# Full attention's value products in two row halves with two banks of sums, and row maxima of two heads at once in the score slots

## The chip, the cores and the metric

The kernel runs on one core of one Trainium2 chip. The metric is the device time of one execution in microseconds, lower is better. Five engines work side by side, each through its own instructions in order: TensorE (PE, matmuls into PSUM), VectorE (DVE), ScalarE (ACT), GpSimd (POOL) and SyncE (SP, which issues most transfers).

## The reference, cut to what matters

Four layers follow each other on x, a 2048 x 512 matrix; each adds its result to x.

```python
x = x + _A_ref(_layernorm(x, axis=-1), A_wq, A_wk, A_wv, A_wo)
x = x + _B_ref(_layernorm(x, axis=-1), B_wq, B_wk, B_wv, B_wo, B_beta)
x = x + _A_ref(...)    # the same two layers once more
x = x + _B_ref(...)
```

Layer A is full attention of 32 heads of 16 channels over all 2048 keys, with one key head and one value head for all of them. Layer B cuts the 2048 positions into four segments of 512; within a segment it does causal attention of 32 heads (p = softmax(logits + mask), a_dot = p @ v), and mixes that with a read from a memory matrix that the earlier segments filled.

## The kernel before, in words

**Layer A.** A unit is four heads (two pairs) of one block of 512 queries, against the 16 tiles of 128 keys; there are 8 units a block, 4 blocks, 2 layers. For each key tile, `a_units` computes the scores of one head pair at a time with `by_pairs` (8 matmuls, 49 rows by 32 columns, heads in the lower and the upper half of the array's rows, each half into a bank of its own), ScalarE takes the exponential of the 128 x 1024 result (L743) into a buffer `pa`, and one key tile later `a_pv` multiplies with the values: four f32 matmuls of 128 rows by 17 columns, one for each head, in four strips of columns, which sum over the key tiles in the one bank `pva`. After a unit's last key tile VectorE transposes `pva` (L772), divides and stores.

**Layer B.** For each segment (a block) and each of 8 units of four heads: `b_inputs` projects queries and keys, `b_rowmax` finds for every query row the maximum of its masked scores (a set: 4 heads by 4 query tiles, of 128 to 512 columns), with VectorE reading the scores from PSUM (L968); `guard_rows` transposes the maxima (L674), scales them and sends them into the query tile, so that they are subtracted in the scores proper. `b_attend` then computes the scores, exponentials (L1007, into `pb`) and value products `b_pv` (sums in the bank `pvb`). The last block of the second layer B uses `b_rowmax_masked`.

**PSUM** has eight banks. `layout` names, for each stage, what is shared out of them: `sc`, pairs of banks for scores ("score slots"), `m`, single banks for row maxima, `r`, single banks for projections and transposes. Each is a `Ring`: jobs take its slots in turn, and a job waits until its slot has been read. While both layers run (stage "ab") there are two score slots, one `m` bank and one `r` bank; `pva` is bank 6 and `pvb` bank 7.

**The order.** All work is written as generators that yield when they next can go on. `weave` runs layer A's units of one block (`a_units`) beside the other layer's work on the block before (`side`), and `par` runs parts of `side` beside each other. They choose by estimated times (`pe`, `on`), with an estimated 130 ns (`DRAIN`) for a change between matmuls of different shapes on the array ("full", "cols", "rows"). A scheduler that keeps close to this order then lays out each engine's instructions. So a change of a cost, of a bank or of a shape's name moves instructions through the whole program.

Of the kernel before, what the change touches and what calls it, by code (L numbers as in the profile page):

```python
# [29 lines left out]
F32 = mybir.dt.float32  # L30
F32R = mybir.dt.float32r
BF16 = mybir.dt.bfloat16
# [3 lines left out]
ALU = mybir.AluOpType  # L36
AX = mybir.AxisListType

P = 128
# [50 lines left out]
def net_kernel(ctx, tc, x_in, a_wq, a_wk, a_wv, a_wo, b_wq, b_wk, b_wv, b_wo, b_beta, cst, out):  # L90
    nc = tc.nc
    V, A, G = nc.vector, nc.scalar, nc.gpsimd
# [3 lines left out]
    def together(first, *a, **k):  # L96

        if first:
            nc.tensor.matmul(*a, **k)  # L99
        else:  # L100
            with tc.high_priority(offset=400):
                tc.keep_in_program_order(nc.tensor.matmul(*a, **k))  # L102
# [52 lines left out]
    def tmp(n, shape, dt, tag):  # L155
        return pools[n].tile(shape, dt, tag=tag, name=nm(tag))
# [93 lines left out]
    xh = st([P, 4, 512], F32R, "xh")  # L250
    xl = st([P, 4, 512], F32R, "xl")
    bank = ps_1.tile([P, 8, 512], F32, tag="bank", name="bank")
    pva, pvb = bank[:, 6, :], bank[:, 7, :]
    V.memset(bank[:, 6:8, :], 0.0)


    srcs = {"Aq": (a_wq, 1), "Ao": (a_wo, 0), "Bq": (b_wq, 1), "Bk": (b_wk, 1), "Bv": (b_wv, 0), "Bo": (b_wo, 0)}
# [446 lines left out]
    def a_units(units):  # L704

        def gate(f, n, k1):
            return 0.0 if f <= phase[0] or (f == phase[0] + 1 and (n == 0 or k1 < 16)) else 1e18

        def load(ui):
            L, _, b, n, _, _ = units[ui]
            return a_load(L, b, n) if L["qr"][b][n // 2] < 1e17 else None

        pend = None
        nxt = load(0)
        for ui, (L, f, b, n, k0, k1) in enumerate(units):
# [12 lines left out]
            for kt in range(k0, k1):  # L730
                pe_, te = [], []
                for u in range(2):
                    yield Need(lambda: max(need, rings["sc"].ready(), L["kr"][kt // 4], gate(f, n, k1)), form)
                    ring = rings["sc"]
                    k, sc = ring.take()
                    ks = L["kst"][:, kt * P:(kt + 1) * P]
                    if L["exact"]:
                        for i in range(2):
                            by_columns(i == 0, sc[:, i, :], ks[0:98], q[0:98, 2 * u + i, :], start=True, stop=True)
                    else:  # L740
                        by_pairs(sc, ks.bitcast(F16), q[:, u, :])
                    x = tmp(4, [P, 2, 512], F32, "pa")
                    A.activation(x, sc, AF.Exp, scale=scale)  # L743
                    ring.free[k] = on("act", pe(432 if L["exact"] else 216, form), 946)
                    pe_.append(x)
                    te.append(ring.free[k] + HOP)
                if kt == k0 + 1 or (kt == k0 and k1 - k0 == 1):
                    nxt = load(ui + 1) if ui + 1 < len(units) else None
                if kt == max(k0, k1 - 3) and (b, n) in L["part"]:
                    L["old"] = tmp(2, [P, 16, 32], F32, "xn")  # L750
                    nc.sync.dma_start(L["old"], L["part"].pop((b, n)))
                if pend is not None:
                    yield Need(lambda: max(pend[-1], pva_free[0] if pend[1] else 0.0), "cols")
                    a_pv(*pend)
                pend = (L, kt == k0, kt, pe_, (f, b, n, k0, k1), kt == k1 - 1, max(te))
        yield Need(lambda: max(pend[-1], pva_free[0] if pend[1] else 0.0), "cols")
        a_pv(*pend)

    a_ob = {}
# [1 line left out]
    def a_pv(L, first, kt, x, unit, last, _):  # L761
        f_, b, n, k0, k1 = unit
        gone[f_] = gone.get(f_, 0) + 1
        t, p = divmod(n, 2)
        for j in (2, 3, 0, 1):
            together(j == 2, pva[32 * j:32 * j + 17, :], lhsT=L["va"][:, kt, 0:17], rhs=x[j // 2][:, j % 2, :],
                     start=first, stop=last)
        e = pe(848, "cols")
        if not last:
            return  # L770
        t1 = tmp(2, [P, 16, 32], F32, "t1")
        V.transpose(t1.rearrange("p a b -> p (a b)"), pva)  # L772
# [171 lines left out]
    def b_rowmax(n, need, exact=False):  # L944

        q, k = (qx, kx) if exact else (qb[n % 3], kb[n % 3])
        m = tmp(2, [P, 4, 4], F32, "m")
        jobs = [[(3, j)] for j in range(4)] + [[(2, j), (0, j)] for j in range(4)] + [[(1, 0), (1, 2)], [(1, 1), (1, 3)]]
        for job in jobs:
            yield Need(lambda: max(need, rings["m"].ready()), "cols" if exact else "rows")  # L950
            ring = rings["m"]
            s, ps = ring.take()
            o_ = 0
            for qt, j in job:
                nk = (qt + 1) * P
                if exact:
                    by_columns(o_ == 0, ps[:, o_:o_ + nk], q[0:96, j, qt * P:(qt + 1) * P], k[0:96, j, 0:nk],
                               start=True, stop=True)
                else:
                    u, i = divmod(j, 2)  # L960
                    by_pairs(ps[:, o_:o_ + nk], q[:, u, qt * P:(qt + 1) * P], k[:, u, 0:nk], 48, (i,))
                o_ += nk
                e = pe(cols(nk), "cols" if exact else "rows")
            o_ = 0
            for qt, j in job:
                nk = (qt + 1) * P
                mo = tmp(1, [P, 512], BF16, "mo")
                V.tensor_tensor_reduce(out=mo[:, 0:nk], in0=ps[:, o_:o_ + nk], in1=maskq[:, 512 - nk:512],  # L968
                                       op0=ALU.add, op1=ALU.max, scale=1.0, scalar=-3.0e38,
                                       accum_out=m[:, j, qt:qt + 1])  # L970
                o_ += nk
                e = on("dve", e, 65 + 1.05 * nk)
            ring.free[s] = e
        yield rings["m"].ready
        gr[n] = guard_rows(m, q, rings["m"], exact)

    b_ob = {}
    pvb_free = [0.0]
# [280 lines left out]
```

## Time and profile before

| | |
|---|---|
| times of three runs | 3223.19, 3226.74 and 3234.41 us; median 3226.74 |
| span of the profiled execution | 3225.5 us (the only time that is known of this execution; it lies among the three) |
| TensorE busy | 2971.5 us, 92% |
| ScalarE busy | 2351.4 us, 73% |
| VectorE busy | 1548.4 us, 48% |
| GpSimd busy | 401.0 us, 12% |
| mean granted TensorE clock | 0.982 |

Busy time counts the time in which at least one instruction of an engine ran. Matmuls overlap, and their ends are modelled, so that the distance from start to start says more of TensorE than its busy time. In the rows of groups, the number behind the bar is the busy time in us, then the mean ns of one instruction, then the idle time of the engine ahead of them and who ended it. In the timeline a row begins with its start and its length in us. In the windows a row has the stretch, its length, then busy time (and count) of PE, PEld, DVE, ACT and POOL, the granted clock, and the DMA's share and rate.

### The profile page before, as it was taken

What the parts mean: (1) busy time and instruction counts of PE and PEld (TensorE: products, weight loads), DVE (VectorE), ACT (ScalarE), POOL (GpSimd) and SP (SyncE); (2) the same over time, 40 slices, a digit from 0 to 9 for tenths busy, and PEclk for the clock granted to TensorE, in tenths of its full rate; (3) what the DMA queues carried; (4) which work ended last, traced back from release to release, by engine and by line L of the source; (5) the groups of instructions that cost most, each with busy time, mean ns of one, the idle gap of its engine ahead of it and who ended that gap; (6) DMA issues with size and microseconds to landing.
All of it is one profiled execution on the core that took longest, in us unless ns stands there. A gap on an engine that the chain in (4) does not pass through costs nothing.

```text
span 3225.5 us, 99506 instructions
## 1 busy us (share of the span) xinstructions
PE 2971.5 (92%) x43522; PEld 1097.9 (34%) x43522; DVE 1548.4 (48%) x4423; ACT 2351.4 (73%) x2583; POOL 401.0 (12%) x569
## 2 busy tenths in 40 slices
PE   6988999999999999999999999899999999999997
PEld 3411333334332343333323323333323233332543
DVE  6601345444554446544455534564446433554365
ACT  3599787866888668876788787777587876888322
POOL 2200111021100220002200011110211012100111
PEclk9999999999999999999999999999999999999968
DMA  4300121022110221102311222221211024210511
GB/s 119 115 25 22 52 60 44 18 73 71 49 41 13 75 86 41 38 22 76 92 41 45 70 80 73 72 55 31 87 48 56 16 78 137 63 42 17 168 51 30
DMA packets 138493, 193.04 MB, mean 60 GB/s; under 512 B 29664, under 2 KB 97088, under 8 KB 138048
## 3 DMA queue, kind: packets, MB, share of 16 engines
q1 hardware_dynamic: 118912, 121.56, 12.8%
q0 software_dynamic: 19136, 65.02, 7.0%
q8 instruction: 343, 5.62, 0.7%
q14 instruction: 102, 0.84, 0.1%
HBM read 126.46 MB, written 60.03 MB: 58 GB/s over the span
## 4 chain that ended last, share of the span: by engine, by line
PE 55%; ACT 25%; issue 7%; DVE 6%; DMA 3%; POOL 2%; SPq 0%; ACTq 0%; POOLq 0%; DVEq 0%
PE bank L99 34%; ACT pa L743 22%; PE bank L441 15%; PE bank L102 5%; ACT pb L1007 3%; POOL w L183 1%; DVE mo L968 1%; PE bank L501 1%; DMA wst<-in_B_wk_dram 1%; DMA wst<-in_B_wv_dram 1%; DVE m L939 0%; DVE w L285 0%; POOL parts L537 0%; DVE qf L519 0%; DVE t L1018 0%
## 5 line engine op out<-in xcount | busy, mean ns | idle before, releaser
L743 ACT ACTIVATE pa<-bank 128x1024 f32<-128x1024 f32 x2048 | 1967.6, 1035 | 476.3 <-PE bank L102 462.3
L99 PE MATMUL bank<-pa,va 128*17 128x512 f32 x2048 | 1063.3, 601 | 46.7 <-ACT pa L743 28.8
L102 PE MATMUL bank<-pa,va 128*17 128x512 f32 x6144 | 1077.1, 601 | 0.0
L99 PE MATMUL bank<-qa,kst 49*32 49x512 f16 x2048 | 713.0, 382 | 89.7 <-ACT pa L743 55.3
L102 PE MATMUL bank<-qa,kst 49*32 49x512 f16 x14336 | 785.1, 386 | 0.7 <-DVE xt L815 0.7
L968 DVE CUSTOM_DVE_ANT_0 mo<-bank,maskq 128x256 bf16<-128x256 f32 (+3 forms) x896 | 436.8, 488 | 454.8 <-PE bank L102 444.3
L1007 ACT ACTIVATE pb<-bank 128x1024 f32<-128x1024 f32 (+2 forms) x384 | 329.0, 882 | 160.3 <-PE bank L102 158.9
L99 PE MATMUL bank<-qkb 48*32 48x128 f16 (+7 forms) x1536 | 374.7, 305 | 56.6 <-DVE m L968 20.5
L102 PE MATMUL bank<-qkb 48*32 48x512 f16 (+7 forms) x6656 | 396.0, 308 | 0.0
L99 PEld LDWEIGHTS <-kst 49*32 49x32 f16 x2048 | 144.8, 89 | 669.2 <-issue 658.7
L441 PE MATMUL bank<-xh,w 128*128 128x512 f32 x832 | 298.0, 419 | 10.3 <-DVE w L315 4.7
L102 PEld LDWEIGHTS <-kst 49*32 49x32 f16 x14336 | 208.9, 89 | 213.8 <-issue 206.7
L183 POOL TENSOR_SCALAR w<-wst 128x512 fp32r<-128x512 f32 x160 | 112.0, 700 | 1200.6 <-PE bank L441 1051.0
L441 PE MATMUL bank<-w,xh 128*128 128x512 f32 x752 | 251.3, 414 | 8.4 <-DVE xl L509 7.4
L99 PEld LDWEIGHTS bank<-pa,va 128*17 128x17 f32 x2048 | 116.9, 95 | 363.0 <-issue 224.4
L99 PEld LDWEIGHTS <-qkb 48*32 48x32 f16 (+1 forms) x1536 | 128.4, 92 | 328.0 <-issue 289.7
L772 DVE STREAM_TRANSPOSE t<-bank 128x512 f32<-128x512 f32 x88 | 62.9, 715 | 338.4 <-PE bank L102 338.1
L441 PEld LDWEIGHTS bank<-xh,w 128*128 128x128 f32 x832 | 161.6, 195 | 80.1 <-issue 35.1
L99 PE MATMUL bank<-pb,vb 128*17 128x512 f32 (+3 forms) x512 | 183.1, 447 | 4.3 <-ACT pb L1007 4.1
L102 PE MATMUL bank<-pb,vb 128*17 128x512 f32 (+3 forms) x1536 | 186.1, 447 | 0.0
L102 PEld LDWEIGHTS <-qkb 50*32 50x32 f16 (+1 forms) x6656 | 144.6, 92 | 103.2 <-issue 100.4
L441 PE MATMUL bank<-xl,w 128*128 128x512 f32 x416 | 169.7, 408 | 0.0
(162 smaller groups left out, 2835.0 us busy)
## 6 DMA issues: line engine op xcount, KB each, us to landing
sb<-parts SPq DMA_DIRECT2D x128, 128.0 KB
qkb<-sb SPq DMA_DIRECT2D x256, 64.0 KB
x<-xt SPq DMA_DIRECT2D x48, 256.0 KB
xt<-x SPq DMA_DIRECT2D x48, 256.0 KB
qa<-sd SPq DMA_DIRECT2D x176, 66.0 KB
wd<-w POOLq DMA_DIRECT2D x20, 512.0 KB, 3.8
w<-wd POOLq DMA_DIRECT2D x18, 512.0 KB, 5.2
xt<-in_A_x_dram SPq DMA_DIRECT2D x32, 256.0 KB
```

The lines of the kernel that those rows point to most:

```text
L99: nc.tensor.matmul(*a, **k)
L102: tc.keep_in_program_order(nc.tensor.matmul(*a, **k))
L183: G.tensor_scalar(o, i, 1.0, 0.0, op0=ALU.mult, op1=ALU.add)
L441: T.matmul(ps, lhsT=l_(kt), rhs=r_(kt), start=n == 0, stop=n == 11)
L501: T.transpose(ps[:, k, :], xn[:, k * P:(k + 1) * P], ident)
L743: A.activation(x, sc, AF.Exp, scale=scale)
L772: V.transpose(t1.rearrange("p a b -> p (a b)"), pva)
L968: V.tensor_tensor_reduce(out=mo[:, 0:nk], in0=ps[:, o_:o_ + nk], in1=maskq[:, 512 - nk:512], op0=ALU.add, op1=ALU.max, scale=1.0, scalar=- ...
L1007: A.activation(e[:, :, 0:w], sc[:, :, 0:w], AF.Exp, scale=0.25 if exact else 0.25 / (UPB * UPB))
```

## The change

It has two parts, and new banks for both. The value products of layer A are split by keys: the upper and the lower 64 rows of a key tile are multiplied by matmuls of their own, eight instead of four, and each half sums in a bank of its own. After the last key tile VectorE copies one bank, adds the other, and transposes the result. The planner counts them as of the scores' shape ("rows"), at 870 ns. The row maxima of layer B are found for the two heads of a pair at once, in a score slot, with five jobs a set instead of ten; VectorE reads each head as before. To make room, stage "ab" has no `m` bank any more, `pva` is banks 6 and 7, `pvb` is bank 5, and the opening ("pa") has two `r` banks instead of three.

```diff
-    pva, pvb = bank[:, 6, :], bank[:, 7, :]
-    V.memset(bank[:, 6:8, :], 0.0)
+    pva, pvb = bank[:, 6:8, :], bank[:, 5, :]
+    V.memset(bank[:, 5:8, :], 0.0)
...
-        sc, m, r = {"a": (3, (), ()), "ab": (2, (4,), (5,)), "b": (2, (4, 6), (5,)), "b0": (0, (4, 6), (5, 0, 1, 2, 3)), "z": (0, (), (5, 4, 6, 0)), "prep": (0, (), (0, 1, 2, 3, 4, 5)), "pa": (2, (), (4, 5, 7))}[kind]
+        sc, m, r = {"a": (3, (), ()), "ab": (2, (), (4,)), "b": (2, (6, 7), (4,)), "b0": (0, (6, 7), (4, 0, 1, 2, 3)), "z": (0, (), (4, 6, 7, 0)), "prep": (0, (), (0, 1, 2, 3, 4, 5)), "pa": (2, (), (4, 5))}[kind]
...
-                yield Need(lambda: max(pend[-1], pva_free[0] if pend[1] else 0.0), "cols")
+                yield Need(lambda: max(pend[-1], pva_free[0] if pend[1] else 0.0), "rows")
...
         for j in (2, 3, 0, 1):
-            together(j == 2, pva[32 * j:32 * j + 17, :], lhsT=L["va"][:, kt, 0:17], rhs=x[j // 2][:, j % 2, :],
-                     start=first, stop=last)
-        e = pe(848, "cols")
+            for h in range(2):
+                w_ = slice(64 * h, 64 * h + 64)
+                together(j == 2 and h == 0, pva[32 * j:32 * j + 17, h, :], lhsT=L["va"][w_, kt, 0:17],
+                         rhs=x[j // 2][w_, j % 2, :], start=first, stop=last)
+        e = pe(870, "rows")
...
         t1 = tmp(2, [P, 16, 32], F32, "t1")
-        V.transpose(t1.rearrange("p a b -> p (a b)"), pva)
-        pva_free[0] = on("dve", e, 602) + HOP
+        ts = tmp(1, [P, 512], F32, "ts")
+        V.tensor_copy(ts, pva[:, 0, :])
+        V.tensor_tensor(ts, ts, pva[:, 1, :], op=ALU.add)
+        pva_free[0] = on("dve", e, 1200) + HOP
+        V.transpose(t1.rearrange("p a b -> p (a b)"), ts)
+        on("dve", 0.0, 602)
...
-        jobs = [[(3, j)] for j in range(4)] + [[(2, j), (0, j)] for j in range(4)] + [[(1, 0), (1, 2)], [(1, 1), (1, 3)]]
+        ring = rings["sc"]
+        if exact:
+            jobs = [[(3, j)] for j in range(4)] + [[(2, j), (0, j)] for j in range(4)] + [[(1, 0), (1, 2)], [(1, 1), (1, 3)]]
+        else:
+            jobs = [[(3, 0)], [(3, 1)], [(2, 0), (0, 0)], [(2, 1), (0, 1)], [(1, 0), (1, 1)]]
...
                 else:
-                    u, i = divmod(j, 2)
-                    by_pairs(ps[:, o_:o_ + nk], q[:, u, qt * P:(qt + 1) * P], k[:, u, 0:nk], 48, (i,))
+                    by_pairs(ps[:, :, o_:o_ + nk], q[:, j, qt * P:(qt + 1) * P], k[:, j, 0:nk], 48)
...
-                mo = tmp(1, [P, 512], BF16, "mo")
-                V.tensor_tensor_reduce(out=mo[:, 0:nk], in0=ps[:, o_:o_ + nk], in1=maskq[:, 512 - nk:512],
-                                       op0=ALU.add, op1=ALU.max, scale=1.0, scalar=-3.0e38,
-                                       accum_out=m[:, j, qt:qt + 1])
+                for i in range(1 if exact else 2):
+                    mo = tmp(1, [P, 512], BF16, "mo")
+                    V.tensor_tensor_reduce(out=mo[:, 0:nk], in0=ps[:, i, o_:o_ + nk], in1=maskq[:, 512 - nk:512],
+                                           op0=ALU.add, op1=ALU.max, scale=1.0, scalar=-3.0e38,
+                                           accum_out=m[:, j if exact else 2 * j + i, qt:qt + 1])
+                    e = on("dve", e, 65 + 1.05 * nk)
...
-        gr[n] = guard_rows(m, q, rings["m"], exact)
+        gr[n] = guard_rows(m, q, ring, exact)
```

More of the change, by code (lines that the diff above doesn't have):

```diff
@@ L752, in a_units @@
                 if pend is not None:
-                    yield Need(lambda: max(pend[-1], pva_free[0] if pend[1] else 0.0), "cols")
+                    yield Need(lambda: max(pend[-1], pva_free[0] if pend[1] else 0.0), "rows")
                     a_pv(*pend)
                 pend = (L, kt == k0, kt, pe_, (f, b, n, k0, k1), kt == k1 - 1, max(te))
-        yield Need(lambda: max(pend[-1], pva_free[0] if pend[1] else 0.0), "cols")
+        yield Need(lambda: max(pend[-1], pva_free[0] if pend[1] else 0.0), "rows")
         a_pv(*pend)
@@ L947, in b_rowmax @@
         m = tmp(2, [P, 4, 4], F32, "m")
-        jobs = [[(3, j)] for j in range(4)] + [[(2, j), (0, j)] for j in range(4)] + [[(1, 0), (1, 2)], [(1, 1), (1, 3)]]
+        ring = rings["sc"]
[3 more added lines that the diff above has]
+            jobs = [[(3, 0)], [(3, 1)], [(2, 0), (0, 0)], [(2, 1), (0, 1)], [(1, 0), (1, 1)]]
         for job in jobs:
-            yield Need(lambda: max(need, rings["m"].ready()), "cols" if exact else "rows")
-            ring = rings["m"]
+            yield Need(lambda: max(need, ring.ready()), "cols" if exact else "rows")
             s, ps = ring.take()
@@ L956, in b_rowmax @@
                 if exact:
-                    by_columns(o_ == 0, ps[:, o_:o_ + nk], q[0:96, j, qt * P:(qt + 1) * P], k[0:96, j, 0:nk],
+                    by_columns(o_ == 0, ps[:, 0, o_:o_ + nk], q[0:96, j, qt * P:(qt + 1) * P], k[0:96, j, 0:nk],
                                start=True, stop=True)
                 else:
-                    u, i = divmod(j, 2)
-                    by_pairs(ps[:, o_:o_ + nk], q[:, u, qt * P:(qt + 1) * P], k[:, u, 0:nk], 48, (i,))
+                    by_pairs(ps[:, :, o_:o_ + nk], q[:, j, qt * P:(qt + 1) * P], k[:, j, 0:nk], 48)
                 o_ += nk
@@ L966, in b_rowmax @@
                 nk = (qt + 1) * P
-                mo = tmp(1, [P, 512], BF16, "mo")
-                V.tensor_tensor_reduce(out=mo[:, 0:nk], in0=ps[:, o_:o_ + nk], in1=maskq[:, 512 - nk:512],
-                                       op0=ALU.add, op1=ALU.max, scale=1.0, scalar=-3.0e38,
-                                       accum_out=m[:, j, qt:qt + 1])
+                for i in range(1 if exact else 2):
[4 more added lines that the diff above has]
+                    e = on("dve", e, 65 + 1.05 * nk)
                 o_ += nk
-                e = on("dve", e, 65 + 1.05 * nk)
             ring.free[s] = e
-        yield rings["m"].ready
-        gr[n] = guard_rows(m, q, rings["m"], exact)
+        yield ring.ready
+        gr[n] = guard_rows(m, q, ring, exact)
     b_ob = {}
```

## The prediction

> **What bounds the kernel now.** I read the page first: the span, the engines' shares, the costliest groups.
>
> ```profile
> span 3225.5 us, 99506 instructions
> PE 2971.5 (92%) x43522; PEld 1097.9 (34%) x43522; DVE 1548.4 (48%) x4423; ACT 2351.4 (73%) x2583; POOL 401.0 (12%) x569
> L743 ACT ACTIVATE pa<-bank 128x1024 f32<-128x1024 f32 x2048 | 1967.6, 1035 | 476.3 <-PE bank L102 462.3
> L99 PE MATMUL bank<-pa,va 128*17 128x512 f32 x2048 | 1063.3, 601 | 46.7 <-ACT pa L743 28.8
> ```
>
> TensorE is busy 92% of the span and ScalarE, which takes the exponentials of layer A, waits 462.3 us for it. A step of layer A over one key tile (a "key tile" below) is two score groups, two exponentials and one value product; there are 2048/2 = 1024. The timeline in a stretch of layer A alone gives the cost of a step.
>
> ```profile
> 1509.52 0.37 PE L99 MATMUL bank<-qa,kst 49*32 49x512 f16 x1
> 1509.86 0.60 PE L99 MATMUL bank<-pa,va 128*17 128x512 f32 x1
> 1509.87 0.62 PE L102 MATMUL bank<-pa,va 128*17 128x512 f32 x3
> 1510.85 0.39 PE L99 MATMUL bank<-qa,kst 49*32 49x512 f16 x1
> 1501.42 0.39 PE L99 MATMUL bank<-qa,kst 49*32 49x512 f16 x1
> 1501.64 0.38 PE L99 MATMUL bank<-qa,kst 49*32 49x512 f16 x1
> 1021.08 0.60 PE L99 MATMUL bank<-pa,va 128*17 128x512 f32 x1
> 1021.96 0.27 PE L99 MATMUL bank<-pb,vb 128*17 128x128 f32 x1
> ```
>
> From start to start a score group takes 0.22 when another follows, 0.34 when a value product does. A value product takes 0.88 before layer B's value product (same shape, 128 rows by 17 columns), 0.99 before scores (49 rows). So a change between the two shapes costs 0.11 each way, and a step costs 2 x 0.22 + 0.88 + 2 x 0.11 = 1.54 us of TensorE. Then the windows view, for a stretch of layer A alone and for one whole block of layer B (835 to 1224 us, cut at the guard transposes L674, one for each half-head unit). The second table counts only instructions on the tile pa.
>
> ```profile
> 155.60:343.60 188.00, 164.70 (x2451) 28.28 (x2449) 22.79 (x48) 187.29 (x204) 2.39 (x4) 1.00 0.09 26
> 835.00:853.90 18.90, 17.36 (x290) 4.62 (x282) 8.89 (x36) 16.84 (x18) 0.00 (x0) 1.00 0.02 3
> 853.90:876.30 22.40, 21.32 (x418) 5.84 (x411) 13.29 (x49) 19.81 (x22) 0.00 (x0) 1.00 0.12 30
> 876.30:906.00 29.70, 28.32 (x489) 11.85 (x485) 19.94 (x61) 21.62 (x25) 4.57 (x6) 1.00 0.20 51
> 906.00:1011.80 105.80, 99.39 (x1869) 33.71 (x1865) 60.50 (x212) 87.53 (x97) 5.64 (x8) 1.00 0.11 31
> 1011.80:1224.00 212.20, 201.22 (x2389) 81.96 (x2385) 98.62 (x234) 147.85 (x163) 41.68 (x56) 0.98 0.23 68
> 853.90:876.30 22.40, 8.38 (x64) 1.06 (x64) 14.84 (x16) 1.00 0.12 30
> 1011.80:1224.00 212.20, 72.49 (x548) 9.16 (x544) 132.44 (x138) 0.98 0.23 68
> ```
>
> Alone, layer A runs at ScalarE's pace: 204 exponentials in 188 us, 1.84 us a key tile. In the block TensorE is busy about 95%, ScalarE 75%, VectorE 52%. A block takes 389 us with 128 key tiles; 138/2 = 69 of them lie in its last 212.2 us, where there are hardly any row maxima, and 16/2 = 8 in the second window.
>
> **Part by part: the value products.** The order of the instructions on TensorE before, at a step in the middle of the program (pa is the exponentials, va the values, kst the keys):
>
> ```order
> L102 MATMUL bank<-qa_26_127,kst_22_119 32x512
> L99 MATMUL bank<-pa_24714,va_24_121 17x512
> L102 MATMUL bank<-pa_24714,va_24_121 17x512
> L102 MATMUL bank<-pa_24692,va_24_121 17x512 x2
> L99 LDWEIGHTS kst_22_119
> ```
>
> These are four products, each over all 128 rows. TensorE at such a step of the changed program:
>
> ```order
> L102 MATMUL bank<-qa_26_127,kst_22_119 32x512
> L99 MATMUL bank<-pa_26868,va_24_121 17x512
> L102 MATMUL bank<-pa_26868,va_24_121 17x512 x3
> L102 MATMUL bank<-pa_26858,va_24_121 17x512 x4
> L99 LDWEIGHTS kst_22_119
> ```
>
> Four products of 128 rows became eight of 64, in the shape of the scores. Counted over the whole order up to the end flag, changes of shape between neighbouring matmuls fall from 3037 to 1646: 1391 x 0.11 = 153 us less on TensorE. About 190 key tiles run alone at ScalarE's pace, where this hides: 190 x 0.22 = 42. On the path: 111.
>
> No row shows eight f32 products of 64 rows. Nearest: four of 128 start one behind another and cover 0.62 where one covers 0.60, and eight f16 score products of half the rows cover 0.22. I take eight as lasting as long as four (0.88), since the halves have their own rows and banks. The upper end is four more starts of 0.007, 1024 x 0.028 = 29 us; a gain below 0.88 is excluded, as every strip of columns still takes the same 512 columns at the same number of passes. The Trainium skill, page "TensorE: Matmul & The Clock Gate", section "Part 3: Packing small matmuls — row/col tiling", gives about 4 ns for each further tile; by it the upper end would be an estimated 16 us instead of 29; the trace shows the larger step.
>
> At the end of each of 88 units VectorE now copies one bank and adds the other before the sums come free, where one transpose did it:
>
> ```profile
> L772 DVE STREAM_TRANSPOSE t<-bank 128x512 f32<-128x512 f32 x88 | 62.9, 715 | 338.4 <-PE bank L102 338.1
> L519 DVE COPY qf<-bank 128x512 f32<-128x512 f32 x91 | 62.8, 690 | 149.4 <-PE bank L441 149.3
> L285 DVE TENSOR_TENSOR w<-wst,w 128x512 fp32r<-128x512 f32 x160 | 112.2, 702 | 97.2 <-POOL w L183 95.9
> L537 POOL TENSOR_SCALAR parts<-qf 128x512 f16<-128x512 f32 x104 | 97.0, 932 | 94.4 <-DVE qf L519 63.6 <-ACT qf L517 17.4 <-DVE mv L477 7.9
> ```
>
> By the copy and addition of this size, 0.69 + 0.70 = 1.39 against 0.72: the sums are free 0.67 later, 88 x 0.67 = 59 us at most. The next unit's first value product is two score groups away, and in the ScalarE-paced stretches TensorE has 0.3 us to spare a step, so I take 5 us. VectorE gets some 120 us more work, at 48% busy.
>
> **The row maxima.** Two heads at once halve their matmuls. One set (four heads, 4 x 1280 columns) takes 5120/512 x 0.22 = 2.2 us of TensorE; 56 of the 64 sets change: 56 x 1.1 = 62 us less. But the results now lie in the two score slots that the exponentials of both layers use, and VectorE still reads each head by itself. What a slot is held for:
>
> ```profile
> 1248.42 0.37 PE L99 MATMUL bank<-qkb 48*32 48x512 f16 x1
> 1248.87 0.69 DVE L968 CUSTOM_DVE_ANT_0 mo<-bank,maskq 128x512 bf16<-128x512 f32 x1 [1.01 <-PE bank L102]
> 1240.24 0.42 DVE L968 CUSTOM_DVE_ANT_0 mo<-bank,maskq 128x256 bf16<-128x256 f32 x1 [0.64 <-PE bank L102]
> 1240.71 0.42 DVE L968 CUSTOM_DVE_ANT_0 mo<-bank,maskq 128x256 bf16<-128x256 f32 x1
> 1241.06 0.08 DVE L968 DVE_READ_ACCUMULATOR2_ANT m<- 128x1 f32 x1
> 1241.19 0.27 PE L99 MATMUL bank<-qkb 48*32 48x256 f16 x1 [0.23 <-DVE m L968]
> L968 DVE CUSTOM_DVE_ANT_0 mo<-bank,maskq 128x384 bf16<-128x384 f32 x224 | 123.5, 551 | 153.2 <-PE bank L102 153.1
> L968 DVE CUSTOM_DVE_ANT_0 mo<-bank,maskq 128x128 bf16<-128x128 f32 x224 | 64.8, 289 | 6.7
> 1251.32 0.39 PE L99 MATMUL bank<-qa,kst 49*32 49x512 f16 x1
> 1251.80 3.78 ACT L743 ACTIVATE pa<-bank 128x1024 f32<-128x1024 f32 x4 [0.28 <-PE bank L102]
> 834.98 0.28 PE L674 MATMUL bank<-cs,m 128*16 128x128 f32 x1
> 835.82 0.27 DVE L679 TENSOR_REDUCE mmx<-bank 16x1 f32<-16x128 f32 x1
> DVE mo L968 <- PE bank L102: 444.3, 429, 7.9
> PE bank L99 <- DVE m L968: 20.5, 36, 3.4
> ```
>
> VectorE starts 0.45 after the matmuls; one head costs it 0.70 at 512 columns, 0.57 at 384, 0.46 at 256, 0.30 at 128 (with the reading of the accumulator), and TensorE follows 0.05 after its end. So the five jobs of a set hold their slots for 0.5 + 2 x 0.70 = 1.9 (twice), 0.5 + 2 x 0.87 = 2.25 (twice) and 0.5 + 4 x 0.46 = 2.35; VectorE needs 8.2 us a set, one after another. A score group holds its slot 0.48 + 1.04 = 1.5. Before, row maxima waited in a bank of their own, and VectorE waited for TensorE (444.3 us), TensorE for VectorE hardly (20.5). The Trainium skill, "TensorEngine Tiling (Array Packing)", section "PSUM Bottleneck", says that tiling speeds TensorE but not the emptying of its banks; by it the 62 us would be worth nothing, where the matmul rows alone count them in full. The trace agrees so far: a set takes VectorE 8.2 us and TensorE 2.2.
>
> The order shows how far this goes. ScalarE before, from the second guard transpose of that block (pb is layer B's exponentials, pa layer A's):
>
> ```order
> L1007 ACTIVATE pb_12339<-bank 128x1024
> L1007 ACTIVATE pb_12357<-bank 128x1024
> L1007 ACTIVATE pb_12375<-bank 128x2x384
> L1007 ACTIVATE pb_12393<-bank 128x2x384
> L1007 ACTIVATE pb_12431<-bank 128x1024
> L1007 ACTIVATE pb_12475<-bank 128x2x256
> L743 ACTIVATE pa_12491<-bank 128x1024
> L743 ACTIVATE pa_12534<-bank 128x1024
> ```
>
> Fourteen more of pa follow up to the third guard transpose. ScalarE after, from the second guard transpose to the third:
>
> ```order
> L1016 ACTIVATE pb_13613<-bank 128x1024
> L1016 ACTIVATE pb_13631<-bank 128x1024
> L1016 ACTIVATE pb_13649<-bank 128x2x384
> L743 ACTIVATE pa_13755<-bank 128x1024
> L743 ACTIVATE pa_13765<-bank 128x1024
> L1016 ACTIVATE pb_13783<-bank 128x2x384
> ```
>
> That is all: two of layer A's exponentials where there were 16. The five windows held 8, 8, 8, 35 and 69 key tiles (rounded), and hold 2, 1, 12, 32 and 81. VectorE before, in the first window of the block, at the end of a set of row maxima (each pair of rows is one head's maximum):
>
> ```order
> L968 ISA mo_12264,m_12011<-bank,maskq_92 128x256
> L968 ISA m_12011 128x1
> L968 ISA mo_12266,m_12011<-bank,maskq_92 128x256
> L968 ISA m_12011 128x1
> L968 ISA mo_12296,m_12011<-bank,maskq_92 128x256
> L968 ISA m_12011 128x1
> ```
>
> The maxima follow one another. VectorE after, in the same window (phk and parts belong to layer B's next inputs):
>
> ```order
> L519 COPY qf_14027<-bank 128x512
> L977 ISA mo_13552,m_13425<-bank,maskq_92 128x128
> L977 ISA m_13425 128x1
> L887 TENSOR_SCALAR phk_14035<-qf_14027 128x512
> L977 ISA mo_13570,m_13425<-bank,maskq_92 128x256
> L977 ISA m_13425 128x1
> L539 SCALAR_TENSOR_TENSOR parts_14029<-qf_14027,parts_14029 128x512
> L977 ISA mo_13572,m_13425<-bank,maskq_92 128x256
> L977 ISA m_13425 128x1
> L889 SCALAR_TENSOR_TENSOR phk_14035<-qf_14027,phk_14035 128x512
> ```
>
> Five passes of 0.7 us (the last, L285, follows) now stand between maxima whose slot everybody waits for, one of them behind GpSimd's 0.93.
>
> **The block followed along the order.** Second window, times from its guard transpose: the guard's slot is read until 1.3 (834.98 to 835.82 + 0.27, above); layer B's scores then take it, their exponential ends at 2.9; first 512 job at 2.9, second at 4.2 behind a value product; the 384 jobs wait for VectorE until 4.8 and 6.35, the 256 job until 8.15, the score groups until 9.95 and 11.75, the next guard for an exponential until 13.3. So 13.3 us, about 4 of them TensorE's work. First window: first job at 4.0, VectorE done 8.2 + 5 x 0.7 + 0.9 after 4.4, layer B's scores behind it at 16.3: 16.8. Third: ScalarE's work, 12 x 1.84 + 4.3 = 26.4, and some 10.5 us around the set in which only one key tile's pair runs, 8.7 lost: with the ends 36.6. Fourth: 32 x 1.84 + 4 x 5.2 + 4 x 8.7 = 114.5; its last window, followed alone, came out 2 under this, so 106.5. Last: 212.2 + 12 more key tiles x 1.32 = 16, less 110 fewer changes of shape, 12, and 3 for the first set: 219. Sum 16.8 + 13.3 + 36.6 + 106.5 + 219 = 392 against 389.
>
> So TensorE's saving in a block (about 25 us) is given back: +3 us a block, seven blocks with row maxima of this kind, +22; the opening, with two instead of three banks for projections and the later sums, +5; the last block's side, 200 us, is unchanged. 3225.5 + 27 = 3253 for the profiled execution, whose span is 1.2 us under the median shown, 3226.74; I carry nothing over for that.
>
> **The rivals.** (A) The slots keep up: other TensorE work lies beside each hold, and the saving stays. 111 + 62 = 173 less, and 20 for later sums and 25 of waiting left: 3225.5 - 128 = about 3100. For it: TensorE is the busiest engine and ScalarE has 25% to spare; a key tile moved to the stretch without row maxima costs 1.32 there. Against: the windows above, and VectorE's strict order. It decides if a set of row maxima costs under some 3 us of waiting instead of the 6 that I find. (B) VectorE's other work delays each set by 3 us more than I followed: 56 x 3 = 168, about 3420. (C) The two row halves of an f32 product run one after the other instead of together: 1024 x 0.88 = 901, near 4120. Against it: the f16 scores' halves do run together, in the same shape. That the order didn't change is excluded, as the pieces show.
>
> **How the numbers follow.** My forecast, 3253, gets 0.54, with a range of its own from 3195 (2 us less a set, half of the followed windows too long) to 3340 (1.5 us more a set, 29 for the starts). A gets 0.34, B 0.08, C 0.04. To hold 8 in 10 the range takes in the forecast's and the larger part of A: 3060 to 3370. What a measurement of this kernel can tell from no change is about 0.3%, 10 us. Faster by more: A, and 0.05 of the forecast's, 0.38. Slower by more: 0.55. Within: 0.07.
>
> **What would show it.** Right: value product to score at 0.88; TensorE waiting for VectorE's maxima at L99 in the hundreds of us where it was 20.5; windows between the first three guard transposes of a block near 17 and 13 us; the last part of a block near 219; ScalarE idle around each set. Wrong: a second window of 9 us or less, a block under 375 us, or a value product over 0.95.

## The result, and the profile after

The changed kernel takes 3679.9 us (median of four runs, 3661.2 to 3692.8), the kernel before 3225.0 beside it: a ratio of 1.1411, interval 1.1363 to 1.1459. The sign was forecast, the size was not: 455 us instead of 27, far above the upper end of the range, 3370. The page of the kernel after (the span; the engines; TensorE's granted clock in 40 slices; the groups of layer A's exponentials and value products) and its cores view:

```profile
span 3678.3 us, 116329 instructions
PE 3098.5 (84%) x51714; PEld 1305.1 (35%) x51714; DVE 1677.1 (46%) x4599; ACT 2350.5 (64%) x2583; POOL 392.7 (11%) x569
PEclk9999998999799997999979999999998999898978
L743 ACT ACTIVATE pa<-bank 128x1024 f32<-128x1024 f32 x2048 | 1968.4, 1047 | 842.0 <-PE bank L102 755.6
L99 PE MATMUL bank<-pa,va 64*17 64x512 f32 x2048 | 1099.9, 618 | 66.0 <-ACT pa L743 41.5
core 0: 3678.3 us, clock 0.931
```

ScalarE does the same work and waits 842 us ahead of layer A's exponentials instead of 476; TensorE's share fell from 92 to 84%. TensorE's busy time rose from 2971.5 to 3098.5 us, where the forecast had it fall. The granted clock was 0.982 before. In the windows view, a stretch of layer A alone, and then one block of layer B at the places of the forecast's five windows (from guard transpose to guard transpose, the last up to the next block):

```profile
173.40:357.70 184.30, 152.44 (x3093) 48.53 (x3091) 32.65 (x61) 179.04 (x195) 2.36 (x4) 1.00 0.09 25
929.10:948.30 19.20, 14.95 (x189) 5.51 (x181) 11.70 (x41) 5.08 (x6) 1.68 (x3) 0.76 0.07 19
948.30:964.70 16.40, 9.56 (x145) 2.79 (x138) 8.88 (x36) 4.87 (x6) 0.35 (x1) 0.50 0.07 18
964.70:1010.20 45.50, 37.89 (x653) 12.40 (x653) 16.34 (x55) 27.75 (x31) 0.00 (x0) 0.80 0.06 15
1010.20:1137.30 127.10, 101.50 (x2048) 39.17 (x2048) 64.34 (x215) 82.18 (x91) 4.76 (x7) 0.95 0.10 29
1137.30:1377.50 240.20, 218.49 (x3430) 101.16 (x3430) 114.64 (x261) 173.73 (x191) 44.28 (x60) 0.99 0.21 63
```

The block takes 448.4 us (forecast 392, before 389). The windows hold 5, 2, 24, 64 and 162 of layer A's exponentials, two for a key tile: the 2, 1, 12, 32 and 81 key tiles of the forecast, in more time. In the third column from the end is the granted clock: before it was 1.00 in the first four of these windows, now 0.76, 0.50, 0.80 and 0.95. What happens in the second window, from the timeline (start, length, engine; in brackets the idle time ahead and who ended it):

```profile
951.82 0.58 PE L99 MATMUL bank<-qkb 48*32 48x512 f16 x1 [1.14 <-ACT pb L1016]
952.38 1.03 PE L99 MATMUL bank<-pb,vb 128*17 128x512 f32 x1
952.62 0.69 DVE L977 CUSTOM_DVE_ANT_0 mo<-bank,maskq 128x512 bf16<-128x512 f32 x1 [2.92 <-PE bank L102]
953.46 0.69 DVE L977 CUSTOM_DVE_ANT_0 mo<-bank,maskq 128x512 bf16<-128x512 f32 x1
956.61 0.52 PE L102 MATMUL bank<-qkb 48*32 48x384 f16 x7 [0.37 <-DVE m L977]
958.36 0.37 PE L99 MATMUL bank<-qkb 48*32 48x256 f16 x1 [1.13 <-DVE m L977]
960.45 0.58 PE L99 MATMUL bank<-qa,kst 49*32 49x512 f16 x1 [1.13 <-DVE m L977]
961.51 1.02 ACT L743 ACTIVATE pa<-bank 128x1024 f32<-128x1024 f32 x1 [9.04 <-PE bank L102]
962.40 0.58 PE L99 MATMUL bank<-qa,kst 49*32 49x512 f16 x1 [0.99 <-DVE m L977]
962.73 0.08 DVE L977 DVE_READ_ACCUMULATOR2_ANT m<- 128x1 f32 x1
```

Both score slots go to row maxima in turn. VectorE reads from 952.62 to 962.81, with one pause of 0.85 us: 9.3 us of reading a set. TensorE waits for it at nearly every job, and ScalarE, which needs a slot with scores, stands still for 9.04 us. The waits over the whole program:

```profile
ACT pa L743 <- PE bank L102: 755.6, 452, 10.8
PE bank L99 <- DVE m L977: 113.5, 129, 3.3
PE bank L99 <- ACT pa L743: 240.2, 579, 4.1
```

### The profile page after: what moved, and what is told of

Its sections match the earlier page's. It is cut to its first block, busy times and chain, and to the rows that moved or that the text cites. A ratio compares the mean times of both kernels' runs of the same rounds, so it can differ in the third digit from the quotient of the medians.

```text
span 3678.3 us, 116329 instructions
## 1 busy us (share of the span) xinstructions
PE 3098.5 (84%) x51714; PEld 1305.1 (35%) x51714; DVE 1677.1 (46%) x4599; ACT 2350.5 (64%) x2583; POOL 392.7 (11%) x569
## 5 line engine op out<-in xcount | busy, mean ns | idle before, releaser
L99 PE MATMUL bank<-pa,va 64*17 64x512 f32 x2048 | 1099.9, 618 | 66.0 <-ACT pa L743 41.5
L102 PE MATMUL bank<-pa,va 64*17 64x512 f32 x14336 | 1146.8, 618 | 0.0
L99 PE MATMUL bank<-qa,kst 49*32 49x512 f16 x2048 | 761.7, 390 | 260.0 <-ACT pa L743 162.3
L102 PE MATMUL bank<-qa,kst 49*32 49x512 f16 x14336 | 827.0, 396 | 8.1 <-DVE m L977 7.0
L102 PEld LDWEIGHTS <-kst 49*32 49x32 f16 x14336 | 241.1, 91 | 556.6 <-issue 545.1
L99 PE MATMUL bank<-qkb 48*32 48x128 f16 (+7 forms) x1088 | 319.9, 332 | 115.1 <-DVE m L977 40.6
L102 PE MATMUL bank<-qkb 50*32 50x512 f16 (+4 forms) x7104 | 344.6, 333 | 23.1 <-DVE m L977 19.7
L99 PEld LDWEIGHTS <-kst 49*32 49x32 f16 x2048 | 181.7, 93 | 495.4 <-issue 479.6
L441 PE MATMUL bank<-xh,w 128*128 128x512 f32 x832 | 315.4, 435 | 14.7 <-DVE w L315 4.8
L102 PEld LDWEIGHTS bank<-pa,va 64*17 64x17 f32 x14336 | 238.7, 95 | 29.6 <-DVE ts L776 12.8
L99 PEld LDWEIGHTS bank<-pa,va 64*17 64x17 f32 x2048 | 175.4, 95 | 207.0 <-ACT pa L743 112.7
L775 DVE COPY ts<-bank 128x512 f32<-128x512 f32 x88 | 60.6, 688 | 352.9 <-PE bank L102 352.6
L102 PE MATMUL bank<-pb,vb 128*17 128x512 f32 (+3 forms) x1536 | 204.7, 475 | 0.0
L99 PE MATMUL bank<-pb,vb 128*17 128x512 f32 (+3 forms) x512 | 198.6, 476 | 1.1 <-ACT pb L1016 1.0
L99 PEld LDWEIGHTS <-qkb 48*32 48x32 f16 (+1 forms) x1088 | 99.5, 98 | 245.5 <-issue 225.2
```

What stands on the lines that cost most here:

```text
L441: T.matmul(ps, lhsT=l_(kt), rhs=r_(kt), start=n == 0, stop=n == 11)
L775: V.tensor_copy(ts, pva[:, 0, :])
```

## The experiments

Each ratio below is to the kernel before, run beside it, with the 95% interval in brackets.

**Each part alone.** The row maxima of two heads in the score slots, with value products and their one bank of sums as before:

```diff
-            yield Need(lambda: max(need, rings["m"].ready()), "cols" if exact else "rows")
-            ring = rings["m"]
+            yield Need(lambda: max(need, ring.ready()), "cols" if exact else "rows")   # ring = rings["sc"]
...
+                    by_pairs(ps[:, :, o_:o_ + nk], q[:, j, qt * P:(qt + 1) * P], k[:, j, 0:nk], 48)
```

> The row maxima alone: two heads at once in the score slots, value products as before. Slots (row maxima in the score slots hold up the exponentials, TensorE falls idle and its granted clock to half): the whole loss is here, 3650 to 3800 us, since the value products' saving of some 111 us is missing too; granted clock near 0.93, the window between the second and third guard transpose of a block near 16 us. Values (the loss comes from the split value products and their later sums): 3200 to 3300 us, clock near 0.98.

Measured: 3647.2 us, ratio 1.1342 (1.1300 to 1.1384). Waits of this kernel:

```profile
ACT pa L743 <- PE bank L102: 823.3, 483, 9.8
PE bank L99 <- DVE m L971: 91.3, 96, 2.1
```

This part alone is 426 us slower, nearly the whole loss. It has the changed kernel's banks too, but the opening with fewer of them is not where it loses: the first guard transpose L674 starts at 449.1 us, before at 450.2. The other part alone: the split value products with two banks of sums, and the row maxima one head at a time. Eight banks don't hold all that, so row maxima, projections and guard rows share one bank:

```diff
+    pva, pvb = bank[:, 6:8, :], bank[:, 5, :]
...
+        if kind == "ab":
+            rings["m"] = rings["r"]
```

> The split value products alone: row maxima one head at a time as before, but in the bank of the projections (stage ab has no bank for them otherwise). Slots: faster than before, 3080 to 3180 us (111 us saved on changes of shape, some lost to the later sums and to the shared bank), clock near 0.98. Values: 3400 us or more.

Measured: 3284.1 us, ratio 1.0215 (1.0176 to 1.0254). It missed, above the 3080 to 3180 that were expected: a gain of TensorE's did not reach the end. What the shared bank costs alone, in the kernel before (the last two lines of that diff only):

> The kernel before, with the row maxima sharing one bank with the guard rows, as in the run of the split value products alone (3284); value products as before, one bank of sums freed by one transpose. If the split saves its 111 us and the late sums cost 38, the shared bank costs the rest: 3284 + 111 - 38 = 3357, at least 3320. If the split's saving does not reach the end: 3221 to 3260, and the split alone brings nothing or a loss.

Measured: 3296.4 us, ratio 1.0239 (1.0189 to 1.0289). This lies between the two expectations. The sharing costs 75 us. The split beside it brings 12, by medians whose intervals overlap. Engines of the kernel with the shared bank alone, and with the split too:

```profile
PE 2997.0 (91%) x43522; PEld 1102.0 (33%) x43522; DVE 1562.3 (47%) x4423; ACT 2353.6 (71%) x2583; POOL 407.3 (12%) x569
PE 2888.2 (88%) x51714; PEld 1293.9 (39%) x51714; DVE 1681.6 (51%) x4599; ACT 2351.2 (72%) x2583; POOL 406.0 (12%) x569
```

TensorE's busy time falls by 109 us (the forecast had 153 less in all, 111 of it on the path); its idle time rises by 95.

**Late sums.** The kernel before, with a copy and a second pass over the bank ahead of the transpose, so that the bank comes free as late as in the changed kernel:

```diff
-        V.transpose(t1.rearrange("p a b -> p (a b)"), pva)
...
+        V.tensor_copy(ts, pva)
+        V.tensor_tensor(ts, ts, pva, op=ALU.max)
...
+        V.transpose(t1.rearrange("p a b -> p (a b)"), ts)
```

> The kernel before, with the value sums freed as late as in the changed kernel: a copy and a second pass (the maximum of the copy and the sums, which changes nothing) ahead of the transpose, 88 times. Slots: 0 to 60 us more than before, 3225 to 3285 us. Values: over 3330 us.

Measured: 3259.2 us, ratio 1.0130 (1.0096 to 1.0165): 38 us, where the forecast took 5 and its bound was 59. The run also gives VectorE two more passes at each of the 88 ends, and does not tell the two apart. The reverse, the split value products with ScalarE copying one bank while VectorE transposes the other:

```diff
-        V.tensor_copy(ts, pva[:, 0, :])
-        V.tensor_tensor(ts, ts, pva[:, 1, :], op=ALU.add)
+        A.copy(ts, pva[:, 0, :])
+        V.transpose(t1.rearrange("p a b -> p (a b)"), pva[:, 1, :])
...
```

> The split value products alone (3284), with the sums freed as early as before: at a unit's end ScalarE copies one bank while VectorE transposes the other, and the rest is done from SBUF. If late sums are what eats the split's saving: 38 us or more less, under 3250. If the shared bank sets the pace, so that TensorE's saving turns into waits elsewhere: 3265 to 3290.

Measured: 3278.1 us, ratio 1.0161 (1.0128 to 1.0194), 6 us under the split alone, which the intervals do not tell apart. So with the shared bank late sums are not what eats the saving. That the bank sets the pace there fits the time, but was not shown by itself. Waits of TensorE in it:

```profile
PE bank L99 <- ACT pa L745: 139.5, 394, 2.6
PE bank L99 <- DVE m L978: 36.1, 63, 3.2
PE bank L99 <- DMA qkb<-sb: 25.2, 16, 3.7
PE bank L902 <- DVE phk L893: 24.9, 15, 2.0
```

With the shared bank alone these were 94.5, 34.0, 20.4 and 10.2 us, so that most of the added waiting is for ScalarE's exponentials of layer A. What TensorE saves there, it waits.

**The planner.** The changed kernel with VectorE's cost of a maximum nearer to the trace (0.80 us at 512 columns instead of 0.60), which reorders the program:

```diff
-                    e = on("dve", e, 65 + 1.05 * nk)
+                    e = on("dve", e, 270 + 1.03 * nk)
```

> The changed kernel, with the planner's estimate of VectorE's time for one head's maximum raised from 65 + 1.05 n to 270 + 1.03 n ns (near the distances in the trace); nothing that is computed changes. Slots: the hold itself is the cost, so the time stays within 3% of the changed kernel, 3600 to 3750 us. Planner (the order is laid for holds that are too short): under 3500 us.

Measured: 3660.1 us, ratio 1.1389 (1.1343 to 1.1436). An order that knows what a maximum costs is hardly better, and the intervals overlap.

**Pairs or slots.** The row maxima in the score slots, but one head a job, ten jobs a set as before:

> The row-maxima part alone, but one head a job as before (ten jobs a set instead of five), still in the two score slots. Sharing the slots as the cause: VectorE reads the same bits in the same order, so about as slow as the pairs, 3600 to 3750, TensorE's 62 us more included. Pairing as the cause (a slot held for two or four maxima instead of one or two): most of the loss goes, 3250 to 3400.

Measured: 3617.5 us, ratio 1.1235 (1.1199 to 1.1272). Sharing the slots is the cause; the pairs make it a little worse (30 us), although they take half of the matmuls. The opposite, pairs outside the score slots: the kernel before, where a pair of maxima takes both of two banks that projections and guard rows use singly.

```diff
+        if kind == "ab":
+            rings["m"] = Both(rings["r"])      # "ab": (2, (), (4, 5)); ready when both are, takes both
```

> The kernel before with the row maxima of two heads at once, in two banks that they share with the projections and guard rows (each of those takes one of the two, a pair of maxima both), and not in the score slots. Taking the score slots as the cause: nothing of the loss is left, and TensorE's 62 us less show in part, 3160 to 3260. Pairs as such, or a bank shared with the projections, as the cause: 3280 to 3400.

Measured: 3244.0 us, ratio 1.0069 (1.0045 to 1.0092). The loss of 426 us is down to 19. A gain from TensorE's 62 us less does not show.

**The length of the reading.** The row maxima alone, with each head's bank read twice:

```diff
+                    for _ in range(1 if exact else 2):
                       V.tensor_tensor_reduce(out=mo[:, 0:nk], in0=ps[:, i, o_:o_ + nk], in1=maskq[:, 512 - nk:512],
```

> The row-maxima part alone (3647), with VectorE reading each head's score bank twice over in the 56 paired sets; a set's reading grows from about 9 to about 18 us, nothing else changes. Slots held by VectorE's serial reading as the cause: the whole of the added reading comes through, 56 x 8 to 9 us, 4080 to 4160. VectorE's other work or the moved order as the cause, with the reading itself mostly covered: under 3800.

Measured: 4149.3 us, ratio 1.2886 (1.2843 to 1.2929): 502 us more than the row maxima alone, 9.0 a set. The engines of the row maxima alone, and with each bank read twice:

```profile
PE 3180.7 (87%) x43522; PEld 1091.5 (30%) x43522; DVE 1559.6 (43%) x4423; ACT 2356.3 (65%) x2583; POOL 393.1 (11%) x569
PE 3343.6 (81%) x43522; PEld 1113.8 (27%) x43522; DVE 1999.3 (48%) x6215; ACT 2360.3 (57%) x2583; POOL 391.6 (9%) x569
```

The ends of one set's reading in the row maxima alone, then in this run (its first two passes and its last row):

```profile
922.85 0.69 DVE L971 CUSTOM_DVE_ANT_0 mo<-bank,maskq 128x512 bf16<-128x512 f32 x1 [5.51 <-PE bank L102]
933.04 0.08 DVE L971 DVE_READ_ACCUMULATOR2_ANT m<- 128x1 f32 x1
1012.36 0.69 DVE L972 CUSTOM_DVE_ANT_0 mo<-bank,maskq 128x512 bf16<-128x512 f32 x1 [6.36 <-PE bank L102]
1013.10 0.69 DVE L972 CUSTOM_DVE_ANT_0 mo<-bank,maskq 128x512 bf16<-128x512 f32 x1
1031.38 0.08 DVE L972 DVE_READ_ACCUMULATOR2_ANT m<- 128x1 f32 x1
```

Without the pauses in between (1.2 and 1.5 us) the set takes 9.1 us and then 17.6, so that VectorE has some 56 x 8.5 = 476 us more to do; by busy time it is 440. All of it is on the path, and some 26 us besides. The other way, a shorter reading: the mask is added by small matmuls, and one pass takes the maxima of both heads.

```diff
-                    by_pairs(ps[:, :, o_:o_ + nk], ..., 48)
+                    by_pairs(ps[:, :, o_:o_ + nk], ..., 48, (0, 1), (maskw, nk - P))
...
+                    V.reduce_max(m[:, 2 * j:2 * j + 2, qt], ps[:, :, o_:o_ + nk], axis=AX.X)
```

> The row-maxima part alone (3647), with a shorter reading: the mask is added by eight small matmuls a query tile, and VectorE takes the maxima of both heads in one pass instead of two passes and two accumulator reads; a set's reading falls from about 9.3 to about 6.4 us, TensorE gets some 0.6 us more. Reading on the path, as with its doubling: 56 x 2.3 to 2.9 us less, 3480 to 3520. A floor under it (the order, the crowding of the slots): over 3580.

Measured: 3425.5 us, ratio 1.0635 (1.0595 to 1.0674). It is below the 3480 to 3520 that were expected. The group of its longest passes, and the eight passes of one set in the timeline, merged into one row:

```profile
L970 DVE TENSOR_REDUCE m<-bank 128x2 f32<-128x1024 f32 x112 | 134.7, 1222 | 223.1 <-PE bank L102 217.5 <-ACT pa L743 4.1 <-ACT pb L1013 1.5
871.92 5.94 DVE L970 TENSOR_REDUCE m<-bank 128x2 f32<-128x1024 f32 x8
```

This set is read in 5.94 us, some 3.1 less than the 9.1 above; 56 of them make about 174 us. The kernel gained 222, more than was taken from VectorE. With this reading, pairs in two banks outside the slots:

> As the run before it, with the shorter reading as well. If the two shared banks are held too long there, it is faster than that run by 20 us or more; if they are not waited for, within 15 us of it or a little slower by the mask's matmuls (56 x 0.6 = 34 us of TensorE at most).

Measured: 3216.0 us, ratio 0.9984 (0.9965 to 1.0003): the best of the versions, and not told apart from the kernel before. It is 28 us faster than the run with the longer reading, which fits two shared banks that are held too long there.

**The clock.** The gain beyond VectorE's time points to TensorE itself. Where the granted clock is 0.50 its work takes longer: layer B's value product at 952.38 above lasts 1.03; a product of that form lasted 0.60 in the rows of before at full clock. Two fillers of about the same length at full clock, written behind each of the 280 paired jobs of the row maxima alone, into a bank that nobody reads. The first, in the shape of the row maxima, uses half of the rows:

```diff
+            for _ in range(0 if exact else 4):
+                by_pairs(bank[:, 7, :], q[:, 0, 0:P], k[:, 0, 0:512], 48, (0,))
```

> The row-maxima part alone (3647), and after each of the 280 paired jobs four more groups of matmuls, 48 rows to 128x512, into a bank that nobody reads, some 0.9 us a job, so that TensorE does not idle while a slot is held. Clock as a cause of the size (TensorE idles on the slots, is granted half its clock, and then its own work takes twice as long): time at half clock falls from about 500 us to under 250, and the kernel falls to 3450 to 3580. Slots alone: time at half clock may fall, but the kernel stays at 3640 or goes up by what filler lies on the path, to at most 3647 + 250.

Measured: 3807.5 us, ratio 1.1825 (1.1782 to 1.1869). The clock fell, to 0.918, where it was to rise, so this run could not give time back by it. The second, f32 products over all rows:

```diff
...
+            for c in (() if exact else (2, 3, 0, 1)):
+                together(c == 2, bank[32 * c:32 * c + 17, 7, :], lhsT=warm[:, 0:17], rhs=warm, start=True, stop=True)
```

> As the run with filler matmuls (3808), with other filler of about the same length: one group of four f32 products, 128 rows by 17 columns, 512 long, after each of the 280 paired jobs, 0.88 us and two changes of shape. The filler of half the rows left the granted clock at 0.918. If the full-height filler keeps the clock up and the clock is a cause of the size: granted clock over 0.95, and the kernel under 3700. If the clock comes up and the time does not fall (3760 to 3880), or the clock stays where it was, a lower clock goes with the waits and adds little.

Measured: 3677.9 us, ratio 1.1398 (1.1351 to 1.1445). Then the second with 256 columns, and with 128:

> As the run with full-height filler (3678, clock 0.979), with 256 columns a product instead of 512, about 0.44 us a job. If the filler's own time is on the path and the clock gives time back: with half the filler and most of the clock, 3540 to 3630, under the row maxima alone (3647). If the clock gives nothing, the filler's cost halves: 3655 to 3670.

> The same with 128 columns a product, about 0.22 us a job. With the clock as a cause: if the clock still stays above 0.965, under the half dose; if it falls back to 0.945, about as the row maxima alone. If the clock gives nothing: 3647 to 3660, whatever the clock.

Measured: 3637.7 us, ratio 1.1278 (1.1240 to 1.1316), and 3629.5 us, ratio 1.1263 (1.1225 to 1.1301). Both lie between the times that the two causes were to give. This filler reads nothing that the jobs make, and in the traces it does not stand behind its jobs. Its rows with 512, 256 and 128 columns (count, shortest, median and longest in ns, first and last start in us):

```profile
L102 PE MATMUL bank<-warm x1680: 592/592/1057, 3.2 to 3156.3; 128*17 128x512 f32 x187
L102 PE MATMUL bank<-warm x1680: 379/379/634, 3.2 to 1948.5; 128*17 128x256 f32 x187
L102 PE MATMUL bank<-warm x1680: 272/273/421, 3.2 to 1347.4; 128*17 128x128 f32 x187
```

VectorE takes the maxima of these jobs from about 425 to 3323 us and later. So with 128 columns the filler is used up early in the third of seven such blocks, and none of the three runs tests filler behind the jobs. The cores view of the row maxima alone; with half-height filler; with full-height filler of 512, 256 and 128 columns; and of the shorter reading:

```profile
core 0: 3642.2 us, clock 0.943
core 0: 3807.0 us, clock 0.918
core 0: 3679.8 us, clock 0.979
core 0: 3633.5 us, clock 0.965
core 0: 3622.7 us, clock 0.958
core 0: 3422.8 us, clock 0.973
```

In steps of 3 us the changed kernel's clock reads 0.50 from 939 to 969 us, 0.89 in the next step, and 1.00 from 972 to 981. If it is one of the two everywhere, the time at 0.50 is 2 x (1 - clock) x span: 415, 624, 155, 254, 304 and 185 us; 116 in the kernel before, 508 in the changed one. No run moves the clock alone. The kernel with 128 columns ends 18 us earlier than without (runs of 3624.6 to 3640.5 against 3643.6 to 3655.9), but the ratios' intervals touch. The first two blocks of the row maxima alone, and of that run, which has most of its filler there:

```profile
449.00:900.00 451.00, 399.75 (x5373) 138.53 (x5366) 190.85 (x555) 292.16 (x318) 49.43 (x69) 0.94 0.15 44
900.00:1351.00 451.00, 398.98 (x5431) 136.97 (x5424) 203.59 (x592) 294.75 (x321) 51.79 (x71) 0.95 0.15 44
449.00:887.00 438.00, 408.49 (x6255) 155.54 (x6254) 190.24 (x555) 291.61 (x318) 50.53 (x70) 1.00 0.16 46
887.00:1338.00 451.00, 418.33 (x6248) 155.26 (x6247) 204.58 (x592) 294.62 (x321) 50.65 (x70) 0.99 0.16 45
```

Some 90 us at half clock are gone from the two, TensorE has the filler more to do, and they are 13 and 0 us shorter; the five behind them differ by 4 us at most.

Three comparisons give a rate. The two long fillers differ by 130 us, with 469 us at half clock between them, 0.28 us for each; but they ran in different places, and the half-height filler's own lengthening is in it. The shorter reading brought some 48 us beyond VectorE's share, with 230 less at half clock, 0.21. With each bank read twice, half clock grew by 664 us and the time by some 26 more than the reading, 0.04. By these rates the 299 us that the row maxima add at half clock would be 12 to 84 of their 426. So TensorE's own work is slower there, but how much of the loss the clock makes stays open.

The Trainium skill, "TensorE: Matmul & The Clock Gate", sections "Part 1: The HAM clock gate" and "Terms", gives two states, half clock after an idle window of about 3.4 us, and a penalty of half the time at half clock; by it 299 us would be at most an estimated 150. The two states agree with the steps of 3 us here. Idle time alone does not explain the half-height filler, whose third window of the same block is

```profile
963.90:1004.50 40.60, 37.50 (x481) 13.18 (x473) 19.08 (x57) 21.02 (x23) 4.98 (x6) 0.83 0.14 38
```

TensorE is busy 92% of it, and the granted clock is 0.83; from 993 to 1002 us it is busy throughout, at 0.50. What in the half-height filler leaves the clock low (rows, type or length of the matmuls) was not tried.

## Why the prediction was wrong

**The value product's length: right.** Forecast 0.88 us from a product to the scores; in the stretch of layer A alone:

```profile
302.20 0.60 PE L99 MATMUL bank<-pa,va 64*17 64x512 f32 x1 [0.32 <-ACT pa L743]
303.07 0.38 PE L99 MATMUL bank<-qa,kst 49*32 49x512 f16 x1
```

0.87 us, for eight products of 64 rows as for four of 128: the halves do run together, and rival C is out.

**111 us on the path: wrong.** Beside a shared bank TensorE's busy time fell by 109, but the end moved by 12; and in the changed kernel the value part, taken on top of the row maxima, costs 33 (3680 against 3647). The forecast set the saving against the span as if TensorE's share of 92% made it the bound of every stretch. Where slots or a bank are waited for, it is not.

**The opening, 5 us with the later sums: mis-sized.** Most of the 33 us lies there. The first guard transpose of the program starts at 486.8 us in the changed kernel, at 449.1 in the row maxima alone, with 8 key tiles more done by then; at 1.84 us each they are 15 of these 38 us. From there to the first guard transpose of the last block it is 3042 us against 3055, about what 8 key tiles fewer save, and from that to the end 150 against 138. Which of fewer banks, later sums and the split makes the opening longer was not tried; the row maxima alone have the fewer banks and no such loss.

**Late sums, 5 us: mis-sized.** In a run of their own they cost 38. The forecast had a bound of 59 and took a small part of it, on the argument that TensorE has time to spare where ScalarE sets the pace; two thirds of the bound came through. In the changed kernel's stretch of layer A alone ScalarE, which was idle for 0.7 of 188 us before, is idle for 5.3 of 184: there is not that much time to spare.

**A slot's holding times and VectorE's 8.2 us a set: mis-sized.** The set above took 9.3: at 512 columns it is 0.84 from the first head of a pair to the second, in the next bank (952.62 to 953.46), where 0.70 was taken. That is 1.1 x 56 = 62 us.

**The block followed along the order: the step that failed.** By windows, forecast and measured: 16.8 and 19.2; 13.3 and 16.4; 36.6 and 45.5; 106.5 and 127.1; 219 and 240.2. The mechanism is there, with the key tiles of the forecast in each window and the waits of TensorE for VectorE that were asked for (113.5 us), but each window is longer: what was followed as covered by other work was not. For the fourth the sum had been 114.5, and 8 us were taken off because one window, followed alone, came out shorter; that correction was wrong. The sum priced TensorE's work there at full clock; it was granted 0.50 to 0.95. And the last part was costed at 1.32 us a key tile, with 12 off for fewer changes of shape: TensorE is busy 218.5 us in it, 17 more than before, and idle for 10.7 more. A block loses 59 us instead of 3. In place of that cover the runs showed that VectorE's reading lies on the path: doubled, it adds 9.0 us a set; shortened by some 3.1, it takes 4.0 a set away.

**The row maxima in sum.** The forecast's 27 in all, without its 106 for the value products, held 133 us for them, TensorE's 62 less included. They cost 426. With the 62 us that TensorE was to save that is 488, where VectorE's reading is 56 x 9.1 = 510: taking slots that two engines share and giving them to a third, which reads serially, cost nearly its whole reading here. The forecast's sign hung on a near balance, 133 against 106, neither of which was met; it came out right because the row maxima were far dearer than either.

**The rivals.** A (the slots keep up) is refuted by the row maxima alone. B was the nearest in kind, with 3 us a set more than followed; it named VectorE's other passes between the maxima. A set of maxima cost (426 - 133) / 56 = 5.2 us more than forecast; the runs put that on the reading itself and, in a part that stays open, on the clock. Whether the other passes add to it was not tried.

## What to carry to other kernels

Before a job is moved into a ring of buffers that feeds the engine which sets the pace, count how long each holds a buffer, over all of its serial readers: here nearly every microsecond of VectorE's reading came out at the end, though VectorE was busy less than half of the span. A saving on the busiest engine is worth its size only in the stretches where nothing else is waited for; look at each stretch's window, not at the share of the whole. And when an engine is made to wait, look at the clock that it is granted there before you price its work by rows from stretches without waits. Look in the trace, too, where an added filler ran: it need not be where it was written.

## What the hardware showed that was not expected

TensorE's granted clock falls to half where it waits for slots (0.50 in the second window): 508 us of the changed kernel by the cores view, 116 before, if the clock is always one of two. Filler of half the array's rows kept TensorE busy but left the clock lower (0.918), filler over all rows brought it to 0.979, though it did not run where it was written. Eight f32 products of 64 rows in two halves take as long as four of 128 (0.87 us). One VectorE pass over 1024 elements in two banks takes 1.22 us, where two passes of 512 with their accumulator reads take 1.54 (952.62 to 954.16).
